# A planner that keeps VectorE's two-operand and double-rate operations apart from GpSimd's, half-height q^T and k^T loads, and other decode priorities

## The chip, the cores and the metric

One core of one Trainium2 chip runs the whole program. The metric is the device time of one execution in microseconds, as the median of three runs. The engines are TensorE (PE for matmuls, PEld for weight loads), VectorE (DVE), ScalarE (ACT) and GpSimd (POOL); SyncE (SP) issues the DMAs.

## The reference

Attention with a memory term, then a two-layer MLP without biases, all in fp32:

```python
B, H, S, D = 8, 8, 576, 64
scores = where(causal, -1e9, q @ k^T / sqrt(D))
a = exp(scores - scores.max(-1));  a /= a.sum(-1) + 1e-9
local = a @ v
phi(x) = where(x > 0, x, exp(x) - 1) + 1
mem = (phi(q) @ M_prev) / (phi(q) @ z_prev + 1e-6)
gate = 1 / (1 + exp(-beta))                     # one number a head
x = (gate * mem + (1 - gate) * local)           # -> 4608 tokens x 512
h = x @ w_in;  g = h - tanh(h);  out = g @ w_out  # w_in 512 x 2048, w_out 2048 x 512
```

## The kernel before

**Attention.** The 64 heads (8 batches of 8) are taken one after the other, t = 0 to 63, in 32 pairs; `EPV = 4`, the first four pairs (heads 0 to 7), use plain fp32 matmuls, the later ones a split of each operand into a rounded high part and a remainder (fp32r), so that a product is two or three fast matmuls. For one head: `scores` makes S = qK^T in four chunks of 128 queries and 192, 320, 448 and 576 keys (PE, line 191, into the PSUM tiles psS and psA); `masked` (DVE, L321) adds the causal mask, writes P and takes the row's extreme into nm; ACT (L223) takes the exponential and sums it into nm. `scale_phi` works on four numbers a row: `nm <- nm,eb` (DVE, L279), `nm <- nm,nr` (DVE, L259) and `rs <- nm` (L329); then two fills `P <- ph,nm` (128x128, DVE or POOL) put the memory term into the same P, so that one product with v and M makes both. `transp` transposes P in blocks (PE, L199), ACT casts the result to pt's high part (L235), DVE subtracts for the remainder (`pt <- psA,pt`, L259); `pv` multiplies by v; `scale_x` and `store_x` scale x^T and write it to DRAM.

For each pair: `load_qk` brings q^T and k^T into qk (head 0 and head 1 side by side; the host has laid the 64 rows of each out twice, on 128 partitions), `qx` and `kx` are the high copies (ACT, DVE or POOL), the lower half of qx (`qx <- qk,qx`, 64x1024) and kz (64x1152) the remainders, `vs` the split of v; `prep_phi` makes ph and nr (`nr <- nr,enbx` among it).

**Weights.** w_in and w_out come as raw 8-byte words and are decoded on the chip in chunks of 512 KB: one `TENSOR_SCALAR` (DVE, L279), two integer `SCALAR_TENSOR_TENSOR` (DVE, L303), an absolute value (ACT L297 or DVE), one more `SCALAR_TENSOR_TENSOR`, then the high copy wi/wo and its remainder. The 14 chunks of the first half of the hidden units (phase A: `FCA = 7` of w_in, 7 of w_out) are decoded during attention, raw data in the buffers xr and ot, temporaries dt and dg; `PRI_I` and `PRI_O` give each chunk's place in units of the head number t. The 18 chunks of the second half (phase B; buffers rawB, tB, gB, two of each) can only start when attention's buffers are released, about 712 us into the span.

**MLP.** `feed(0)` does phase A for 12 blocks of 384 tokens, laid between the heads (`LAG = 20`, `PACE = 5`); `feed(1)` does phase B alone after it. In a block, x is split (`xh` the copy, `xl <- xr,xh` the remainder, 128x384 four times); each of the 7 or 9 hidden units of 128 is 12 matmuls into psM, a tanh on ACT, `g <- psM,t` on DVE, the copy gh and the remainder `gl <- g,gh`; then 3 output tiles of 21 or 27 matmuls each.

**The order.** All of this is recorded as a list of operations with options (engine, modelled cost, the call). `Plan.run` builds the order: `_schedule` steps a model clock and gives each engine the ready operation of best rank; `_latest` runs the result backwards to get the next ranks; of `PASSES = 4` the best is written out as the instruction streams. Where an operation may run on several engines, DVE is charged `BIAS = 1000` ns. The model's numbers set only the order and the engine of each operation; on the chip each engine runs its stream in order and waits by semaphores.

## Time and profile before

| quantity | before |
|---|---|
| median of 3 runs (lowest to highest) | 1264.38 us (1262.83 to 1265.12) |
| profiled execution | 1263.97 us |
| its span, first to last instruction | 1262.1 us |
| mean granted PE clock | 0.992 |
| busy: PE, DVE, ACT, POOL | 1197.9, 794.8, 680.3, 644.4 us |

The span has five stages that the text below uses: 0 to 90 us (heads 0 to 7, plain fp32), 90 to 374 us (heads 8 to 35, with 9 of the 14 decoded chunks and the first phase-A work), 374 to 712 us (heads 36 to 63 with most of phase A), 712 to 840 us (the rest of phase A and the decoding for phase B), 840 us to the end (phase B). A PE that is busy is not yet a PE at its best, because matmul ends are modelled; its waits are listed by what released them.

### The profile page before, as it was taken

To read this page: it belongs to the slowest core of one execution; us is meant where nothing else is said; L and a number is where in the kernel's file an instruction comes from. 1 tells how busy PE (TensorE), PEld (TensorE's weight loads), DVE (VectorE), ACT (ScalarE), POOL (GpSimd) and SP (SyncE) were. 2 spreads that over 40 slices of the span, in tenths; PEclk is the share of its full clock that TensorE was granted. 3 is DMA by queue.
4 is the path that set the end of the run, shared out by engine and by line. 5 is a ranking of instruction groups with operands and counts; after the bars stand their busy time and mean duration, and the time that the engine had idled before them with its cause. 6 is when DMAs were issued, how large, how long until landed. Compare 5 with 4: busy or idle time off the path is not lost.

```text
span 1262.1 us, 18668 instructions
## 1 busy us (share of the span) xinstructions
PE 1197.9 (95%) x6496; PEld 1045.3 (83%) x6496; DVE 794.8 (63%) x1663; ACT 680.3 (54%) x1523; POOL 644.4 (51%) x655
## 2 busy tenths in 40 slices
PE   7998778999999999999999989899999999999998
PEld 4457667978898988898989877789999888999987
DVE  4789999999988897887986588622221222222121
ACT  4778766878876776676765445423332222333221
POOL 2548887867755565665656256533332223333221
PEclk9999889999999999999999999999999999999999
DMA  5655535455343343353330354202212221221200
GB/s 175 191 182 162 167 119 186 130 163 159 116 165 114 115 145 115 88 167 118 120 110 22 141 168 167 84 31 70 75 53 74 76 67 34 76 75 51 75 25 26
DMA packets 71999, 138.85 MB, mean 110 GB/s; under 512 B 18272, under 2 KB 42848, under 8 KB 71904
## 3 DMA queue, kind: packets, MB, share of 16 engines
q1 hardware_dynamic: 71904, 137.65, 33.8%
q8 instruction: 51, 0.84, 0.3%
q14 instruction: 44, 0.36, 0.1%
HBM read 109.32 MB, written 28.31 MB: 109 GB/s over the span
## 4 chain that ended last, share of the span: by engine, by line
PE 44%; DVE 7%; issue 1%; DMA 1%; ACT 1%; POOL 0%; SPq 0%; DVEq 0%; ACTq 0%
PE psM L191 41%; PE psA L191 2%; PE psA L199 1%; DVE tB L303 1%; DVE gB L303 1%; DMA rawB<-in_moe_w_in_dram 1%; DVE g L259 1%; DVE pt L259 1%; DVE tB L279 0%; DVE xl L259 0%; DVE P L321 0%; PE psS L191 0%; DMA vm<-in_vm_dram 0%; DVE gl L259 0%; ACT gB L297 0%
## 5 line engine op out<-in xcount | busy, mean ns | idle before, releaser
L191 PE MATMUL psM<-xh,wi 128*128 128x384 f32 x1536 | 414.9, 340 | 7.2 <-DVE g L259 6.3
L264 POOL TENSOR_TENSOR gl<-g,gh 128x384 fp32r<-128x384 f32 x161 | 171.4, 1065 | 327.8 <-ACT gh L235 326.4
L191 PE MATMUL psM<-wo,gh 128*128 128x512 f32 x1008 | 323.1, 396 | 0.8 <-DVE g L259 0.8
L191 PEld LDWEIGHTS psM<-xh,wi 128*128 128x128 f32 x1536 | 278.7, 188 | 12.2 <-DVE g L259 9.2
L191 PE MATMUL psM<-xl,wi 128*128 128x384 f32 x768 | 259.3, 338 | 0.0
L223 ACT ACTIVATE t<-psM 128x384 f32<-128x384 f32 x192 | 93.8, 490 | 249.2 <-PE psM L191 248.9
L191 PEld LDWEIGHTS psM<-wo,gh 128*128 128x128 f32 x1008 | 187.6, 189 | 36.1 <-DVE g L259 1.5
L259 DVE TENSOR_TENSOR g<-psM,t 128x384 f32<-128x384 f32 x192 | 105.7, 551 | 168.5 <-ACT t L223 168.4
L191 PE MATMUL psM<-wo,gl 128*128 128x512 f32 x504 | 199.4, 396 | 6.1 <-DVE gl L259 6.1
L223 ACT ACTIVATE P<-P,nm 128x448 f32<-128x448 f32 (+3 forms) x256 | 157.6, 617 | 41.9 <-DVE nm L321 41.3
L199 PE MATMUL psA<-ident,P 128*128 128x128 f32 x874 | 142.3, 281 | 14.3 <-DVE pt L259 6.5
L199 PEld LDWEIGHTS psA<-ident,P 128*128 128x128 f32 x874 | 107.1, 143 | 47.9 <-issue 12.8
L191 PEld LDWEIGHTS psM<-xl,wi 128*128 128x128 f32 x768 | 144.6, 188 | 1.2
L191 PE MATMUL psA<-pt,vs 128*128 128x512 f32 (+3 forms) x560 | 136.5, 351 | 7.3 <-DVE pt L259 4.3
L259 DVE TENSOR_TENSOR pt<-psA,pt 128x512 fp32r<-128x512 f32 x224 | 133.9, 610 | 6.9 <-ACT pt L235 6.4
L259 DVE TENSOR_TENSOR ot<-psM,pin 128x512 f32<-128x512 f32 x36 | 24.9, 692 | 178.1 <-PE psM L191 178.1
L235 ACT CAST pt<-psA 128x512 fp32r<-128x512 f32 x224 | 116.5, 531 | 35.9 <-PE psA L199 34.4
L235 ACT CAST gh<-g 128x384 fp32r<-128x384 f32 x144 | 73.9, 513 | 85.4 <-DVE g L259 85.0
L191 PEld LDWEIGHTS psM<-wo,gl 128*128 128x128 f32 x504 | 95.2, 189 | 26.2 <-DVE gl L259 7.8
L191 PEld LDWEIGHTS psA<-pt,vs 128*128 128x128 f32 x560 | 93.9, 192 | 19.9 <-DVE pt L259 7.1
L321 DVE CUSTOM_DVE_ANT_0 P<-psS,mask 128x576 f32<-128x576 f32 (+1 forms) x96 | 67.5, 703 | 20.9 <-PE psS L191 20.5
L321 DVE CUSTOM_DVE_ANT_0 P<-psA,mask 128x320 f32<-128x320 f32 (+2 forms) x160 | 68.8, 453 | 18.2 <-PE psA L191 16.7
(155 smaller groups left out, 1858.8 us busy)
## 6 DMA issues: line engine op xcount, KB each, us to landing
qk<-in_qk_dram SPq DMA_DIRECT2D x61, 576.0 KB, 4.0
xr<-xs SPq DMA_DIRECT2D x23, 768.0 KB, 4.4
qn<-in_qn_dram SPq DMA_DIRECT2D x32, 320.0 KB, 3.1
vm<-in_vm_dram SPq DMA_DIRECT2D x30, 320.0 KB, 3.4
part<-ot SPq DMA_DIRECT2D x12, 768.0 KB, 4.1
pin<-part SPq DMA_DIRECT2D x12, 768.0 KB, 5.8
out_dram<-ot SPq DMA_DIRECT2D x11, 768.0 KB, 4.2
rawB<-in_moe_w_in_dram SPq DMA_DIRECT2D x9, 512.0 KB, 3.8
```

Source lines behind the costliest of these rows:

```text
L191: [("PE", n * c / 2.4 + 13, lambda: nc.tensor.matmul(real(out), lhsT, rhs, start=start, stop=stop))],
L199: [("PE", self._n(out) * 2 / 2.4 + 3, lambda: nc.tensor.transpose(real(out), in_, ident))],
L223: [("ACT", c, lambda: nc.scalar.activation(out=out, in_=real(in_), func=func, **kw))],
L235: "ACT", n / 1.2 + (51 if ps else 93), lambda: nc.scalar.copy(out, real(in_))
L259: lambda: nc.vector.tensor_tensor(out=out, in0=real(a), in1=b, op=op),
L264: lambda: nc.gpsimd.tensor_tensor(out=out, in0=a, in1=b, op=op),
L303: [("DVE", self._n(out) / 0.96 + 65, lambda: nc.vector.scalar_tensor_tensor(out=out, in0=real(a), scalar=s, in1=b, op0=op0, op1=op1))],
L321: [("DVE", self._n(out) / 0.96 + 77, lambda: nc.vector.tensor_tensor_reduce(out=real(out), in0=real(in_), in1=mask, scale=-scale, scalar=3 ...
```

## The change

1. In the planner, a resource "port" is added. Every POOL option holds it, and every DVE option that reads more than one SBUF operand of more than one element a row, or that is a copy, a tensor-scalar or an absolute value with its source in SBUF (`fast`). An operation that needs the port is not placed while another one holds it, in the forward and in the backward pass. BIAS stays.
2. `load_qk` for pairs 0 to 3 brings 64 rows a head in two DMAs (head h on partitions 64h to 64h+63, 64x576 each) in place of one of 128x1152; `scores` reads the head's own partitions. The ring `r_qe` becomes four half tiles of qk; a part of ot is no longer used for it, and pair 4 uses the common ring.
3. `PRI_I` and `PRI_O`, the places of the phase-A chunks, become earlier, and the raw buffers of phase A alternate strictly between xr and ot.

```diff
-PRI_I = (-1.0, -1.0, 8.0, 11.2, 12.0, 12.8, 13.6)
-PRI_O = (10.0, 10.3, 10.6, 10.9, 11.2, 11.5, 11.8)
+PRI_I = (-1.0, -1.0, 3.0, 4.0, 5.0, 6.0, 7.0)
+PRI_O = (7.5, 8.0, 8.5, 9.0, 9.5, 10.0, 10.5)
...
-    def add(self, opts, reads, writes, tail=0.0):
+    def add(self, opts, reads, writes, tail=0.0, fast=False):
...
+        sb = sum(not isinstance(x, View) and x.space != DRAM and self._n(x) > 1 for x in reads)
+        opts = [
+            o + (o[0] == "POOL" or (o[0] == "DVE" and (fast or sb > 1)),) for o in opts
+        ]
...
-        self.add(opts, r, [out])
+        self.add(opts, r, [out], fast=a.space != PSUM)
...
                         best = min(
-                            max(free[x[0]], now) + x[1] + self.bias.get(x[0], 0.0)
-                            for x in op["opts"]
+                            max(free[x[0]], free["port"] if x[3] else 0.0, now) + x[1]
+                            + self.bias.get(x[0], 0.0) for x in op["opts"]
                         )
...
-                    take = self._fits(op, now)
+                    take = None if o[3] and free["port"] > now else self._fits(op, now)
...
                     end = free[e] = now + o[1]
+                    if o[3]:
+                        free["port"] = end
...
-    r_raw.t = r_xr.t + (r_xr.t + r_ot.t) * FCA
+    r_raw.t = r_xr.t + r_ot.t
...
-    r_qe.t = r_qk.t + [r_ot.t[0][:, 0:2 * S].rearrange("p (h s) -> p h s", h=2)]
+    r_qe.t = [t[:, h] for t in r_qk.t for h in range(2)]
...
-        d["raw"] = (r_qe if pr <= EPV else r_qk).next()
-        pl.dma(d["raw"], qk[b, p, :, w], False)
+        if pr < EPV:
+            d["raw"] = r_qe.next()
+            for h in range(2):
+                a = slice(64 * h, 64 * h + 64)
+                pl.dma(d["raw"][a], qk[b, p, a, w, h], False)
+        else:
+            d["raw"] = r_qk.next()
+            pl.dma(d["raw"], qk[b, p, :, w], False)
...
-            terms = ((qx[0:64, h], kx[0:64, h]),)
+            a = slice(64 * h, 64 * h + 64)
+            terms = ((qx[a], kx[a]),)
```

The order on SP at the start of the program, before; qk_111 and qk_112 are the two buffers for q^T and k^T:

```order
L673 DMA bt<-in_beta_dram 128x8
L336 DMA qk_111<-in_qk_dram 128x1152
L336 DMA qk_112<-in_qk_dram 128x1152
L336 DMA qn_109<-in_qn_dram 128x640
L336 DMA z_121<-in_z_prev_dram 128x128
L336 DMA vm_110<-in_vm_dram 128x640
L336 DMA ot_169<-in_qk_dram 128x1152
```

and after:

```order
L690 DMA bt<-in_beta_dram 128x8
L341 DMA qk_111<-in_qk_dram 64x576 x2
L341 DMA qn_109<-in_qn_dram 128x640
L341 DMA z_121<-in_z_prev_dram 128x128
L341 DMA qk_111<-in_qk_dram 64x576 x2
L341 DMA xr_159<-in_moe_w_in_dram 128x4x256
L341 DMA vm_110<-in_vm_dram 128x640
```

The k^T of the first pair is now issued sixth and seventh, behind qn and z, where it was third; a raw chunk of w_in goes out ahead of v.

The order on DVE around the first P of the 17th head (psS,mask 128x576), before; dt and dg are the decode's temporaries, xr and ot its raw data:

```order
L303 SCALAR_TENSOR_TENSOR dt_165<-dg_166,dt_165 128x512
L279 TENSOR_SCALAR nm_148<-nm_148,eb 128x4
L279 TENSOR_SCALAR dt_164<-ot_169 128x512
L321 ISA P_145,nm_147<-psS,mask 128x576
L321 ISA nm_147 128x1
L259 TENSOR_TENSOR nm_148<-nm_148,nr_129 128x4
L303 SCALAR_TENSOR_TENSOR dg_166<-ot_169,dt_164 128x512
L259 TENSOR_TENSOR xT_144<-psA_154,tmp_151 64x512
L329 RECIPROCAL rs_150<-nm_147 128x4
L303 SCALAR_TENSOR_TENSOR dt_164<-ot_169,dg_166 128x512
```

and after:

```order
L326 ISA P_145,nm_147<-psS,mask 128x576
L326 ISA nm_147 128x1
L326 ISA P_145,nm_147<-psA_155,mask 128x192
L326 ISA nm_147 128x1
L326 ISA P_145,nm_147<-psA_155,mask 128x320
L326 ISA nm_147 128x1
L264 TENSOR_TENSOR pt_116<-psA_153,pt_115 128x512
```

No decode operation is left between this head's operations. Counted by the number of heads whose 128x576 operation stands ahead of a chunk's first operation, the 14 chunks start at 3 5 6 7 8 10 12 14 14 15 15 15 16 17 before and at 2 2 3 4 5 7 8 8 10 10 12 13 14 15 after: eight of them stood at 12 to 17 heads, now four do. Over the whole program DVE has 1589 rows where it had 1665, ACT 1303 (1269), POOL 702 (660), SP 376 (368), PE the same 6354. To POOL go 40 `xl`, so that all 92 are there, 19 `P <- ph,nm`, so that all 128 are there, 7 gl and 6 kz; 8 of the qx remainders go from POOL to DVE, and a few dozen copies (vs, qx, xh, gh) from POOL to ACT.

The order on DVE in the transition at 712 us, before; rawB, tB and gB belong to phase B's decoding, g to phase A:

```order
L259 TENSOR_TENSOR g_163<-psM_156,t_161 128x384
L279 TENSOR_SCALAR tB_6681<-rawB_6679 128x512
L303 SCALAR_TENSOR_TENSOR gB_6683<-rawB_6679,tB_6681 128x512
L303 SCALAR_TENSOR_TENSOR tB_6681<-rawB_6679,gB_6683 128x512
L259 TENSOR_TENSOR g_162<-psM_157,t_160 128x384
L303 SCALAR_TENSOR_TENSOR tB_6681<-gB_6683,tB_6681 128x512
L279 TENSOR_SCALAR tB_6682<-rawB_6680 128x512
L259 TENSOR_TENSOR g_163<-psM_156,t_161 128x384
```

and after:

```order
L264 TENSOR_TENSOR g_162<-psM_157,t_160 128x384
L264 TENSOR_TENSOR g_163<-psM_156,t_161 128x384
L308 SCALAR_TENSOR_TENSOR tB_6690<-gB_6692,tB_6690 128x512
L284 TENSOR_SCALAR tB_6689<-rawB_6687 128x512
L284 TENSOR_SCALAR tB_6690<-rawB_6688 128x512
L308 SCALAR_TENSOR_TENSOR gB_6691<-rawB_6687,tB_6689 128x512
L308 SCALAR_TENSOR_TENSOR gB_6692<-rawB_6688,tB_6690 128x512
L308 SCALAR_TENSOR_TENSOR tB_6689<-rawB_6687,gB_6691 128x512
L308 SCALAR_TENSOR_TENSOR tB_6690<-rawB_6688,gB_6692 128x512
L308 SCALAR_TENSOR_TENSOR tB_6689<-gB_6691,tB_6689 128x512
L308 SCALAR_TENSOR_TENSOR tB_6690<-gB_6692,tB_6690 128x512
L284 TENSOR_SCALAR tB_6689<-rawB_6687 128x512
```

Decode operations that stood one or three at a time between two g now stand in runs of two chunks, mostly where PE works on output tiles and no g is due. Before, all 18 chunks began ahead of phase A's last tile; now the last of them begin when phase B's first block has begun.

## The prediction

> **What bounds the kernel now.** I read the page's slices first, then the span cut into its five stages, then PE's waits in each stage, and last the durations of single operations on the engine that those waits name.

> ```profile
> PE   7998778999999999999999989899999999999998
> DVE  4789999999988897887986588622221222222121
> PEclk9999889999999999999999999999999999999999
> ```

> PE is the fullest engine nearly everywhere; DVE is full only from slice 4 to 11, where the granted clock dips as well. The stages (columns: length, then busy us of PE, PE weight loads, DVE, ACT, POOL, then granted clock, DMA share, GB/s):

> ```profile
> 0.00:90.00 90.00, 81.05 (x315) 43.46 (x315) 59.62 (x159) 58.88 (x134) 40.35 (x60) 1.00 0.57 179
> 90.00:374.00 284.00, 255.18 (x1516) 221.07 (x1516) 271.04 (x613) 216.93 (x501) 212.56 (x210) 0.97 0.49 154
> 374.00:712.00 338.00, 327.13 (x1969) 296.49 (x1968) 272.15 (x625) 229.41 (x535) 191.72 (x209) 0.99 0.34 108
> 712.00:840.00 128.00, 116.16 (x580) 103.08 (x579) 90.42 (x115) 59.46 (x116) 73.32 (x58) 1.00 0.41 138
> 840.00:1262.00 422.00, 418.33 (x2122) 381.17 (x2121) 101.54 (x154) 115.63 (x238) 126.41 (x119) 1.00 0.18 59
> ```

> In the last stage PE is busy 418.3 of 422 us: nothing but fewer or faster matmuls shortens it, and the change leaves the matmuls as they are. In the second, 90 to 374 us, DVE is busy 271.0 of 284 us, 95%, and PE loses 28.8; in the third DVE is at 80.5% and PE loses 10.9. What PE waits for in the second stage (PE tile, line, releaser: total us, times, longest; 12 rows that add to 28.2):

> ```profile
> PE psA L199 <- DVE pt L259: 5.5, 6, 1.5
> ...
> PE psA L199 <- DVE P L259: 1.9, 1, 1.9
> ...
> PE psS L191 <- POOL P L264: 0.6, 1, 0.6
> ```

> Nearly all of it is DVE, and spread over many tiles: DVE is short of time as a whole. Why it is so full stands in the durations of its smallest work (shortest/median/longest ns):

> ```profile
> L279 DVE TENSOR_SCALAR nm<-nm,eb x64: 208/230/3027, 17.5 to 697.5; 128x4 f32<-128x4 f32 x64
> L259 DVE TENSOR_TENSOR nm<-nm,nr x64: 142/165/1682, 21.3 to 697.7; 128x4 f32<-128x4 f32 x64
> L303 DVE SCALAR_TENSOR_TENSOR nr<-nr,enbx x32: 131/161/1805, 20.8 to 661.9; 128x10 f32<-128x10 f32 x32
> L259 DVE TENSOR_TENSOR g<-psM,t x192: 491/557/560, 102.6 to 1240.6; 128x384 f32<-128x384 f32 x192
> L264 POOL TENSOR_TENSOR qx<-qk,qx x21: 2357/2401/3415, 94.0 to 649.8; 64x1024 fp32r<-64x1024 f32 x21
> L259 DVE TENSOR_TENSOR xl<-xr,xh x40: 519/1002/1372, 204.6 to 1203.3; 128x384 fp32r<-128x384 f32 x40
> L264 POOL TENSOR_TENSOR xl<-xr,xh x52: 1002/1028/2189, 202.9 to 1204.2; 128x384 fp32r<-128x384 f32 x52
> ```

> An operation on four numbers a row that takes 0.2 us at best takes up to 3.0, about as long as POOL's longest operations (2.4 us, at worst 3.4). `g`, with one operand in PSUM, never exceeds 0.56 us in 192 cases. So DVE operations of the class that the change marks "port" stand still while POOL works, and the time counts as DVE busy. In the second stage the groups average (busy us, mean ns):

> ```profile
> L279 DVE TENSOR_SCALAR nm<-nm,eb 128x4 f32<-128x4 f32 x28 | 19.3, 688 | 0.3
> L259 DVE TENSOR_TENSOR nm<-nm,nr 128x4 f32<-128x4 f32 x28 | 14.4, 513 | 0.0
> L303 DVE SCALAR_TENSOR_TENSOR dt<-dg,dt 128x512 f32<-128x512 f32 x10 | 8.8, 878 | 0.0
> L303 DVE SCALAR_TENSOR_TENSOR nr<-nr,enbx 128x10 f32<-128x10 f32 x14 | 7.4, 527 | 0.0
> L303 DVE SCALAR_TENSOR_TENSOR dg<-xr,dt 128x512 int32<-128x512 int32 x5 | 5.4, 1070 | 0.0
> L303 DVE SCALAR_TENSOR_TENSOR dt<-xr,dg 128x512 int32<-128x512 int32 x5 | 5.0, 1008 | 0.0
> L279 DVE TENSOR_SCALAR dt<-xr 128x512 int32<-128x512 int32 x5 | 3.2, 637 | 0.0
> ```

> Standing still costs (688-208)x28 = 13.4, (513-142)x28 = 10.4 and (527-131)x14 = 5.5: 29 us from these three groups alone.

> **The change part by part.** *Port in the planner, second stage.* The model now places such an operation when POOL is free, and moves two-operand work (40 xl, 19 P fills, 7 gl and 6 kz in the whole program) to POOL. On the chip the two streams keep only their order, and durations differ from the model's, so they drift: I take two thirds of the 29 us, 20. A decoded chunk costs DVE 637 + 1070 + 1008 + 878 ns = 3.6 us, and three of the nine leave this stage by the new priorities: 11 us. DVE falls from 271 to 240 us. The PE loss at a given DVE load is read from the two stages: 28.2 us of 284 (9.9%) at 95.4% and 10.9 of 338 (3.2%) at 80.5%, 0.45 points a point. With a length of 273 the load is 87.9%, the loss 6.5% or 17.8 us, and 284 - 28.2 + 17.8 = 273.6 closes the circle: -10 us. What would be late next is PE's own 255.8 us, so this term lies between 0 (DVE's relief is not where PE waits) and -28.

> *The clock in the second stage.* The lowest slices are in the stretch where eight of the fourteen chunks were decoded:

> ```profile
> 120.00:140.00 20.00, 16.70 (x96) 13.23 (x94) 19.94 (x45) 16.49 (x38) 18.51 (x15) 0.92 0.62 192
> 140.00:160.00 20.00, 15.50 (x84) 12.66 (x84) 19.94 (x39) 14.45 (x31) 16.13 (x15) 0.91 0.61 184
> 160.00:180.00 20.00, 15.52 (x70) 12.42 (x71) 19.98 (x38) 12.38 (x26) 16.78 (x13) 0.83 0.46 142
> ```

> DVE has 0.02 to 0.06 us free of 20 there, PE is busy 75 to 84% by modelled ends, and the clock is 0.83 to 0.92. With 3% of 284 us missing in the stage's mean clock, 8.5 us is the most that a full clock could give, 0 the least. The drops go with the decode bunch, which is thinned from eight chunks to four but not gone; I take -2, near the lower end, since the rows at 0.91 and at 0.83 have the same PE load, so load alone does not set it. [...]

> *First stage.* The three chunks put 11 us more on DVE in 0 to 90, which is busy 59.6 of 90 us. PE's waits there (first and last of 3 rows, 8.9 us together):

> ```profile
> PE psS L191 <- DMA qk<-in_qk_dram: 7.0, 1, 7.0
> ...
> PE psA L199 <- DVE xT L259: 0.4, 1, 0.4
> ```

> Only 1.9 us of these are DVE's, so its 30 us of slack cover the chunks on average; if the cover is gone where a chunk falls ahead of a head's P, up to one chunk, 3.6 us, shows. The 7.0 us before the first matmul is a load:

> ```profile
> L336 SPq DMA_DIRECT2D qk<-in_qk_dram x61: 327/333/547, 1.2 to 631.8; - x61
> ```

> An issue takes SP 0.33 us. k^T is now the sixth and seventh issue where it was the third, so it leaves 4 x 0.33 = 1.3 us later, with half the bytes in each. The halved bytes can give back at most some of the 7.0 us. I set the stage at 0, between -4 and +4. That pairs 0 to 3 have four half tiles lets a k load go earlier; PE does not wait for any qk load after the first, so it is 0.

> *Third stage.* The largest of its 6 rows of PE waits, and the last:

> ```profile
> PE psS L191 <- DVE nm L321: 6.1, 5, 3.0
> ...
> PE psA L199 <- DVE xT L259: 0.2, 1, 0.2
> ```

> No chunk is decoded here, so only the port acts: between 0 and -10.9; by the same two thirds of the one DVE-late group, -4.

> *Transition, 712 to 840 us.* PE waits 11.8 us, all for DVE, and DVE's decoding stands still too: (1179 - 683) x 18 = 8.9 us for one of its four operations (whole-run shortest, median, longest; then the stage's busy and mean):

> ```profile
> PE psM L191 <- DVE g L259: 6.0, 9, 1.2
> PE psM L191 <- DVE gl L259: 5.8, 3, 2.0
> L303 DVE SCALAR_TENSOR_TENSOR gB<-rawB,tB x18: 683/1351/1662, 719.0 to 804.4; 128x512 int32<-128x512 int32 x18
> L303 DVE SCALAR_TENSOR_TENSOR gB<-rawB,tB 128x512 int32<-128x512 int32 x18 | 21.2, 1179 | 0.2
> ```

> The three gl that PE waited for go to POOL, and the decode runs stand where no g is due. Against it, the last chunks start after phase B's first block has begun, so their wo may be late for its output tiles. Between -11.8 and +8 (two chunks of 3.6 us, which nothing hides then); I take -4, the gl row less what POOL's slower gl gives back.

> *Phase B.* All xl on POOL: one takes 1.03 us where DVE's median is 1.00, four a block of about 35 us of PE work, and PE has no listed wait in this stage: 0.

> Sum: 0 - 10 - 2 - 4 - 4 + 0 = -20 us. The profiled execution took 1263.97 us, 0.4 under the median, for a span of 1262.1; 1263.97 - 20 = 1244. With half and one and a half times of it this gives 1254 and 1234.

> **The rivals.** *Relief is complete.* If DVE keeps ahead of PE everywhere, 28.2 + 10.9 + 11.8 = 50.9 us go: 1213. For it: these waits are short, so a little slack could end many at once. Against: at 80.5% DVE load PE still lost 10.9 us.

> *The planner's apartness does not last on the chip.* Streams drift, stretched operations stay as they are, and only the 11 us of moved chunks count: DVE at 260 of 280 us, loss 8.7%, -4: 1260. For it: the three small groups stand behind other DVE work in an in-order stream and start when that ends, not when POOL pauses. The stretch is then also partly what hides POOL's time.

> *The transition pays.* As the forecast, but with +8 in place of the -4 there: 1244 + 12 = 1256. For it: wo's chunks are now the last to be decoded. Against: PE waited for no wo before.

> *Slower: POOL becomes late.* All 128 `P <- ph,nm` are on POOL, two a head, behind xl, kz or qx of 1.0 to 2.4 us in its in-order stream, and transposes of P wait for them. In 56 heads a mean delay of 20/56 = 0.36 us a head cancels the gain; at 0.5 us, half an xl, it is 28 us, or 1244 + 28 = 1272. For it: POOL gets more work, and DVE did 19 fills at 0.29 us median where POOL needs 0.40:

> ```profile
> L264 POOL TENSOR_TENSOR P<-ph,nm x109: 389/402/1516, 22.1 to 698.3; 128x128 f32<-128x128 f32 x109
> L259 DVE TENSOR_TENSOR P<-ph,nm x19: 229/291/1300, 197.0 to 689.4; 128x128 f32<-128x128 f32 x19
> POOL gl L264 <- ACT gh L235: 326.4, 103, 18.5
> ```

> Against it: PE waited for a POOL fill once, 0.6 us, though POOL did 109 of them, and POOL stands 326 us of the run waiting only for gh, so it has room. [...]

> **How the numbers follow.** A change of 0.2% (2.5 us) is about what can be told from none. The forecast has 0.48 (1244, own range 1234 to 1254), complete relief 0.10 (1213), the paying transition 0.08 (1256), lost apartness 0.19 (1260, with a spread that puts 0.06 of it within 0.2% of before), POOL late 0.15 (1272). Faster: 0.48 + 0.10 + 0.08 + 0.13 = 0.79; the same 0.06; slower 0.15. The range goes from 1213, which keeps the complete case, to 1267, the unrelieved sum with the first stage's +4 (1264 + 4, rounded down), and leaves out most of the slower case.

> **What would show it.** Right: in the second stage DVE busy near 240 us with `nm <- nm,eb` at a mean of about 0.37 us, PE waits of about 18 us, phase B unchanged at 422 us, and no xl above 1.1 us in the median. Wrong: those small operations still at 0.6 us or more (drift), PE waiting for POOL's P or kz (POOL late), PE waiting for woB or wo remainders at the start of phase B (transition), or a first matmul more than 2 us later than before.

## The result, and the profile after

The changed kernel takes 1234.67 us (median of 4 runs, 1231.45 to 1236.06) against 1264.75 us: a ratio of 0.9761, 95% interval 0.9739 to 0.9783, or 30 us. Forecast were 1244 us, with 1213 to 1267 as the range. The profiled execution, the slowest of the four, took 1236.06 us for a span of 1234.3 us.

The page's slices of the kernel after:

```profile
PE   8998889989999999999999999999999999999998
DVE  5889989889798778786876557721122111122111
PEclk9999989989999999999999999999999999999999
```

DVE no longer stands at 9 from slice 4 to 11 (counted from 1), but the clock row has dips as before. The stages, with the columns of the same view before (length; busy us of PE, PE loads, DVE, ACT, POOL; clock, DMA share, GB/s). To compare work with work, the bounds here are landmarks, events of PE that every run has: the end of the 128x576 scores of head 8 and of head 36, the last transpose, the first of the 2268 matmuls of phase B:

```profile
0.00:86.70 86.70, 81.58 (x317) 43.90 (x318) 64.28 (x168) 62.94 (x144) 38.57 (x54) 1.00 0.61 176
86.70:364.90 278.20, 254.08 (x1497) 221.18 (x1496) 247.86 (x578) 220.79 (x506) 194.14 (x201) 0.95 0.46 146
364.90:693.50 328.60, 324.86 (x1979) 297.63 (x1979) 246.88 (x604) 236.75 (x550) 210.18 (x241) 0.99 0.36 115
693.50:783.90 90.40, 88.53 (x441) 78.78 (x441) 58.89 (x79) 46.43 (x91) 56.01 (x47) 1.00 0.49 168
783.90:1234.30 450.40, 446.64 (x2269) 407.07 (x2268) 97.96 (x160) 131.55 (x269) 160.45 (x157) 1.00 0.18 61
```

By the same landmarks the kernel before has 89.6, 284.3, 336.6 and 101.9 us, and phase B takes 445.9 us of matmuls before and 446.6 after. So 3 us went in the first stage, 6 in the second, 8 in the third, 11.5 in the transition: less than a quarter of the gain is where DVE was fullest.

Even these 6 us are not a shorter stage. At head 36 PE ran 7.5 us ahead of DVE after the change, and 19 matmuls fewer stand in its second stage (1497, before 1516), 18 more in its third (1979, before 1961). Counted from DVE's first P to first P, with nearly the same work in each, the second stage is 1.5 us longer, 284.1 to 285.6, and heads 36 to 63 take 305.0 us where they took 320.3. PE's waits after, in the second stage (10 rows, 23.7 us together; 28.2 before):

```profile
PE psA L204 <- DVE pt L264: 8.7, 5, 3.3
PE psA L196 <- DVE xT L264: 3.7, 4, 1.5
...
PE psA L196 <- DVE pt L264: 0.4, 1, 0.4
```

They are fewer (22, before 33), but the longest is longer than before (3.3 us, 1.9 before). In the third stage and in the transition nearly nothing is left (3.8 and 1.6 us; 10.9 and 11.8 before). All rows, the first three of the third stage, the last two of the transition:

```profile
PE psA L196 <- DVE pt L264: 2.5, 1, 2.5
PE psM L196 <- DVE g L264: 1.0, 1, 1.0
PE psS L196 <- DVE nm L326: 0.3, 1, 0.3
PE psM L196 <- DVE g L264: 1.2, 2, 0.7
PE psM L196 <- ACT ot L240: 0.4, 1, 0.4
```

### The profile page after: what moved, and what is told of

Same layout as the page of the kernel before. It is cut to its first block, busy times and chain, and to the rows that moved or that the text cites. A ratio compares the mean times of both kernels' runs of the same rounds, so it can differ in the third digit from the quotient of the medians.

```text
span 1234.3 us, 18697 instructions
## 1 busy us (share of the span) xinstructions
PE 1195.7 (97%) x6496; PEld 1048.6 (85%) x6496; DVE 715.9 (58%) x1587; ACT 698.5 (57%) x1557; POOL 659.4 (53%) x697
## 3 DMA queue, kind: packets, MB, share of 16 engines
q1 hardware_dynamic: 72032, 135.29, 34.1%
## 4 chain that ended last, share of the span: by engine, by line
PE 84%; DVE 9%; ACT 2%; issue 2%; DMA 1%; POOL 1%; SPq 0%; ACTq 0%; DVEq 0%; POOLq 0%
PE psM L196 58%; PE psA L196 14%; PE psA L204 8%; PE psS L196 4%; DVE nm L284 2%; DVE pt L264 1%; DVE tB L308 1%; DVE P L326 1%; DVE xT L264 1%; DVE qx L264 1%; ACT P L228 1%; DVE g L264 1%; DMA qk<-in_qk_dram 1%; DMA rawB<-in_moe_w_in_dram 1%; DVE dt L308 0%
## 5 line engine op out<-in xcount | busy, mean ns | idle before, releaser
L269 POOL TENSOR_TENSOR gl<-g,gh 128x384 fp32r<-128x384 f32 x168 | 177.9, 1060 | 309.2 <-ACT gh L240 290.5
L264 DVE TENSOR_TENSOR g<-psM,t 128x384 f32<-128x384 f32 x192 | 106.2, 553 | 184.6 <-ACT t L228 182.2
L264 DVE TENSOR_TENSOR pt<-psA,pt 128x512 fp32r<-128x512 f32 (+1 forms) x224 | 135.6, 616 | 26.2 <-ACT pt L240 25.0
L240 ACT CAST pt<-psA 128x512 fp32r<-128x512 f32 (+1 forms) x224 | 116.3, 531 | 54.3 <-PE psA L204 47.4
L264 DVE TENSOR_TENSOR ot<-psM,pin 128x512 f32<-128x512 f32 x36 | 24.9, 691 | 185.5 <-PE psM L196 185.5
L240 ACT CAST gh<-g 128x384 fp32r<-128x384 f32 x150 | 77.1, 514 | 75.9 <-DVE g L264 75.6
L196 PEld LDWEIGHTS psM<-wo,gl 128*128 128x128 f32 x504 | 95.4, 189 | 18.3
L269 POOL TENSOR_TENSOR xl<-xr,xh 128x384 fp32r<-128x384 f32 x92 | 95.2, 1048 | 4.7 <-ACT xh L240 4.5
L269 POOL TENSOR_TENSOR P<-ph,nm 128x128 f32<-128x128 f32 x128 | 59.6, 484 | 59.7 <-DVE nm L264 26.6
```

Of the source, the lines that this page charges most:

```text
L196: [("PE", n * c / 2.4 + 13, lambda: nc.tensor.matmul(real(out), lhsT, rhs, start=start, stop=stop))],
L240: "ACT", n / 1.2 + (51 if ps else 93), lambda: nc.scalar.copy(out, real(in_))
L264: lambda: nc.vector.tensor_tensor(out=out, in0=real(a), in1=b, op=op),
L269: lambda: nc.gpsimd.tensor_tensor(out=out, in0=a, in1=b, op=op),
```

## The experiments

All times are medians of 4 to 15 runs. Stage lengths by the same landmarks, from one profiled execution each (for e12 the fastest of its four, 1206.6 us); the last two columns are PE's waits in the second stage and the time at half rate in it, in us:

| kernel | median us | ratio to before | to head 8 | heads 8 to 36 | to last transpose | transition | waits | half rate |
|---|---|---|---|---|---|---|---|---|
| before | 1264.75 | 1 | 89.6 | 284.3 | 336.6 | 101.9 | 28.2 | 17.1 |
| after | 1234.67 | 0.976 [0.974, 0.978] | 86.7 | 278.2 | 328.6 | 90.4 | 23.7 | 27.3 |
| e1 port alone | 1245.02 | 0.984 [0.983, 0.985] | 88.5 | 295.4 | 321.0 | 90.4 | 31.7 | 34.1 |
| e2 decode alone | 1271.62 | 1.006 [1.004, 1.007] | 85.4 | 296.7 | 337.1 | 103.3 | 36.1 | 17.1 |
| e3 loads alone | 1261.24 | 0.998 [0.997, 0.999] | 90.9 | 279.8 | 335.6 | 103.4 | 31.3 | 6.8 |
| e4 after, latency 260 | 1216.22 | 0.961 [0.960, 0.963] | 85.3 | 264.9 | 320.5 | 90.8 | 14.5 | 6.8 |
| e5 choice alone | 1257.90 | 0.995 [0.993, 0.997] | 93.3 | 274.4 | 334.3 | 102.3 | 25.6 | 17.1 |
| e6 apart alone | 1234.03 | 0.976 [0.975, 0.978] | 86.5 | 275.3 | 328.5 | 90.3 | 23.8 | 20.5 |
| e7 before, latency 260 | 1270.59 | 1.005 [1.003, 1.007] | 86.0 | 294.2 | 334.7 | 104.5 | 32.3 | 23.9 |
| e8 after, nm on ACT | 1207.03 | 0.955 [0.953, 0.957] | 88.1 | 255.2 | 322.9 | 90.6 | 10.1 | 0 |
| e9 e8, latency 260 | 1212.22 | 0.958 [0.956, 0.959] | 83.7 | 266.5 | 320.3 | 90.6 | 13.5 | 10.2 |
| e10 before, nm on ACT | 1269.95 | 1.004 [1.003, 1.005] | 92.1 | 287.8 | 335.1 | 103.6 | 30.8 | 19.3 |
| e11 after, qx and kz cut | 1213.89 | 0.959 [0.958, 0.961] | 82.5 | 266.1 | 322.2 | 90.4 | 12.7 | 10.2 |
| e12 e8 and e11 | 1211.51 | 0.956 [0.954, 0.958] | 87.4 | 256.5 | 320.1 | 90.4 | 14.2 | 3.4 |

Two things stand in this table. The transition is 90.3 to 90.8 us in every kernel whose planner keeps port operations apart and 101.9 to 104.5 in every other; the third stage 320 to 329 against 334 to 337. The second stage runs from 255 to 297 us in no such order, and the first from 82.5 to 93.3. But the second stage's length less the waits and less half of the half-rate time (granted clock 0.50 in the windows below) is 240 to 252 us in all fourteen: 284.3 - 28.2 - 8.5 = 247.6 before, 278.2 - 23.7 - 13.7 = 240.8 after, 264.9 - 14.5 - 3.4 = 247.0 in e4, 255.2 - 10.1 - 0 = 245.1 in e8.

**e1, the port rule alone.**

```diff
 # before, with add(), _schedule and _latest of the change
 PRI_I = (-1.0, -1.0, 8.0, 11.2, 12.0, 12.8, 13.6)
 r_raw.t = r_xr.t + (r_xr.t + r_ot.t) * FCA
 d["raw"] = (r_qe if pr <= EPV else r_qk).next()
```

> Before, with the planner's port resource alone (the decode priorities, raw buffers and q, k loads as before). Theory A, the port rule makes the gain of the third stage (320.3 to 305.0 us between the first P of head 36 and of head 63) and of the transition (101.9 to 90.4 us between the last transpose and phase B): 1264.8 - 15 - 11 = about 1238, with the first stage at 90 us as before. Rival B, the decode priorities make it by clearing DVE early, so that all later work is less pressed: no more than 10 us here, above 1254. Rival C, any new order of this planner moves the time by tens of us at random: no forecast, anywhere from 1230 to 1270.

1245.0 us. Its third stage and transition (the last two of these windows; the first is heads 8 to 36):

```profile
88.50:383.90 295.40, 262.98 (x1526) 229.85 (x1525) 253.77 (x603) 230.83 (x524) 213.04 (x212) 0.94 0.48 149
383.90:704.90 321.00, 320.11 (x1959) 293.87 (x1958) 242.18 (x586) 231.21 (x541) 215.32 (x236) 1.00 0.35 112
704.90:795.30 90.40, 88.55 (x442) 78.77 (x441) 58.77 (x79) 46.46 (x91) 56.02 (x47) 1.00 0.49 167
```

The gain of both later stages is there: the transition takes the 90.4 us of the kernel after, and between the DVE landmarks named in the expectation it is 305.0 us, as there. So B falls: the priorities are not needed for it. The total missed the 1238 by 7, all of it in the second stage, which is 11 us longer than before at a clock of 0.94.

**e2, the decode priorities alone.**

```diff
-PRI_I = (-1.0, -1.0, 8.0, 11.2, 12.0, 12.8, 13.6)
+PRI_I = (-1.0, -1.0, 3.0, 4.0, 5.0, 6.0, 7.0)
-PRI_O = (10.0, 10.3, 10.6, 10.9, 11.2, 11.5, 11.8)
+PRI_O = (7.5, 8.0, 8.5, 9.0, 9.5, 10.0, 10.5)
-r_raw.t = r_xr.t + (r_xr.t + r_ot.t) * FCA
+r_raw.t = r_xr.t + r_ot.t
```

> Before, with the new decode priorities and the alternating raw buffers alone. Theory A: the chunks leave the crowded stretch at 120 to 175 us, the second stage gains up to 5 us, the third stage and the transition stay at 320 and 102 us: 1258 to 1266. Rival B: 1240 to 1250, with the later stages shorter too. Rival C: anywhere.

1271.6 us: slower, outside A's range and far from B's. The later stages stayed, as A said; the second stage grew by 12 us where it was to gain up to 5.

**e3, the 64-row loads alone.**

```diff
-        d["raw"] = (r_qe if pr <= EPV else r_qk).next()
-        pl.dma(d["raw"], qk[b, p, :, w], False)
+        if pr < EPV:  # two DMAs, head h on partitions 64h to 64h + 63
...
-            terms = ((qx[0:64, h], kx[0:64, h]),)
+            terms = ((qx[a], kx[a]),)
```

> Before, with the 64-row q and k loads of the first four pairs alone. If the 1.9 us by which the first matmul came earlier after the change (5.1 us, before 7.0) is the smaller first load, it is here too, and the first P of head 8 comes at 86 to 88 us, not 90: 1260 to 1263 in all. If it came from the order of the other loads, the first stage stays at 90 us and the time at 1264 to 1265. Rival C: anywhere.

1261.2 us. The first wait of PE in e1, which has the old loads, and in e3:

```profile
PE psS L196 <- DMA qk<-in_qk_dram: 7.0, 1, 7.0
PE psS L191 <- DMA qk<-in_qk_dram: 5.0, 1, 5.0
```

The half-height load lets the first matmul start 2 us earlier. That head 8 comes earlier by it was wrong: it came at 90.9 us, 1.3 later than before, with 84.2 us of PE work ahead of it where there were 80.7. The time fell into the forecast range all the same, by a second stage 4.5 us shorter, which nothing in this edit was to change: the number came out, its reason did not.

One reading of the start order, that the first pair's k^T is issued later, was wrong. The loads of 64x576 bring one head's q^T or k^T each, and the first two are the first head's q^T and k^T (kernel after: start, us, engine, operation):

```profile
1.19 1.22 SPq L341 DMA_DIRECT2D qk<-in_qk_dram  x2
3.55 1.11 SPq L341 DMA_DIRECT2D qk<-in_qk_dram  x2
5.12 2.25 PE L196 MATMUL psS<-qk 64*128 64x288 f32 x4 [5.12 <-DMA qk<-in_qk_dram]
```

The first two have landed at 4.25 and 4.98 us and the first matmul waits for these alone; the sixth and seventh issue, the second head's q^T and k^T, land at 7.4 and 8.2 us. So the first head's k^T is still issued third, with half the bytes, and was not put off.

**e4, another order and nothing else.**

```diff
-LAT = 250.0
+LAT = 260.0
```

> After, with the planner's modelled latency between engines at 260 ns in place of 250: nothing of the change is touched, only ties and near ties in the order fall out another way. Theory A: 1230 to 1240, with the second stage up or down by the chance places of its half-rate clock windows (3.4 us each, 8 after, 5 before). Rival C: over 10 us away from 1234.7.

1216.2 us, 18 us faster than the kernel after by 10 ns in a model constant. It is neither A (1230 to 1240) nor a chance of the whole order: transition and phase B stayed within 0.4 us, and heads 36 to 63 take 304.3 us from first P to first P (305.0 after). The first stage differs by 1.4 us; the rest is the second stage, with 1538 matmuls in 264.9 us where the kernel after has 1497 in 278.2, and the clock at 0.99:

```profile
85.30:350.20 264.90, 249.87 (x1538) 220.71 (x1538) 239.60 (x587) 228.94 (x522) 202.96 (x208) 0.99 0.52 161
```

**e5 and e6, the port in the engine choice alone, and in the placing alone.** e5 takes out the two places that hold an operation back, e6 the one that weighs engines:

```diff
 # e5
-                    take = None if o[3] and free["port"] > now else self._fits(op, now)
+                    take = self._fits(op, now)
-                    while heaps[e] and port[heaps[e][0][1]] and free["port"] > now:
+                    while False and heaps[e]:
 # e6
-                            max(free[x[0]], free["port"] if x[3] else 0.0, now) + x[1]
+                            max(free[x[0]], now) + x[1]
```

> After, but the planner looks at the port only when it weighs the engines of one operation against each other; it may place a port operation while another holds the port, forward and backward. Theory A1, keeping apart makes the gain: the third stage is back near 318 us and the transition near 102, where the change alone had 305 and 90; about 1255 to 1265, give or take the second stage's 15. Theory A2, the engine choice makes it: 305 and 90 stay, 1220 to 1240.

> After, but the port is left out where the planner weighs the engines of one operation against each other; it still places no port operation while another holds the port. A1: third stage 305, transition 90 us, 1220 to 1245 by the second stage's chance. A2: 318 and 102, above 1250.

A1 holds in both: e6 is the kernel after (1234.0), e5 has the stages of before (third stage and transition):

```profile
367.70:702.00 334.30, 326.25 (x1961) 294.71 (x1959) 268.01 (x619) 230.24 (x536) 193.05 (x210) 0.99 0.34 107
702.00:804.30 102.30, 90.03 (x442) 78.60 (x441) 83.87 (x104) 48.36 (x94) 61.60 (x47) 1.00 0.48 162
```

DVE's 268 and 84 us there stand against 247 and 59 after.

What the two runs separate is the places in the planner's code, not two effects on the chip. The rule in the placing does two things at once: it keeps port operations apart, and as DVE is held back it moves operations to POOL. All eight kernels with that rule have all 92 xl, 128 fills and 168 gl on POOL; the six without it, e5 too, have 39 to 41 xl, 13 to 21 fills and 7 to 10 gl on DVE. Whether the gain is that DVE has less to do or that the rest is undisturbed needs a kernel with the engines of after and no holding back. None was run.

**e7, before with the latency at 260 ns.** The same edit as e4, in the kernel before.

> Before, with the planner's modelled latency at 260 ns in place of 250. If only the second stage depends on the chance of the order (it went from 265 to 297 us in the runs so far), the third stage stays at 318 to 321 us and the transition at 102 to 104, and the time is 1250 to 1280. If the whole order is a matter of chance (rival C), the third stage or the transition moves by more than 5 us.

1270.6 us, with 294.2 us in the second stage, here 10 us in the other direction. The third stage is 318.0 us between DVE's landmarks, as forecast, and the transition 104.5, half a microsecond over; the first stage moved too, by 3.6 us. So the early stages are open to chance and the later ones are not. The -30 us of the change thus hold a draw on each side: with 260 ns in both planners the same change is worth 54 us (1270.6 to 1216.2). What both pairs show is the third stage by DVE's landmarks (-15.3 and -13.7) and the transition (-11.5 and -13.7), 27 us together each time.

**e8, nm <- nm,eb on ACT.** One of the waits that the second stage kept, in the timeline after (start, us, engine, operation; in brackets the wait ahead of it):

```profile
249.02 3.50 POOL L269 TENSOR_TENSOR kz<-qk,kx 64x1152 fp32r<-64x1152 f32 x1
250.04 4.00 DVE L284 TENSOR_SCALAR nm<-nm,eb 128x4 f32<-128x4 f32 x1
252.49 1.52 POOL L269 TENSOR_TENSOR vs<-vm,vs 128x640 fp32r<-128x640 f32 x1
253.96 0.54 DVE L264 TENSOR_TENSOR pt<-psA,pt 128x384 fp32r<-128x384 f32 x1
254.65 1.09 PE L204 MATMUL psA<-ident,P 128*128 128x128 f32 x4 [2.93 <-DVE pt L264]
```

A product of four numbers a row stands through two POOL operations, pt behind it in DVE's stream is late, and PE waits 2.9 us. The operation becomes ready when ACT's last exponential ends, and in the second stage it fared worse than before, while the other two small groups fared better (kernel after, second stage; 688, 513 and 527 ns before):

```profile
L284 DVE TENSOR_SCALAR nm<-nm,eb 128x4 f32<-128x4 f32 x27 | 23.9, 884 | 1.4 <-ACT P L228 1.4
L264 DVE TENSOR_TENSOR nm<-nm,nr 128x4 f32<-128x4 f32 x27 | 8.2, 303 | 0.0
L308 DVE SCALAR_TENSOR_TENSOR nr<-nr,enbx 128x10 f32<-128x10 f32 x13 | 2.2, 172 | 0.1
```

```diff
-        pl.ts(sm, sm, 1e-9, eb[:, hh:hh + 1], ALU.add, ALU.mult)
+        pl.ts(sm, sm, eb[:, hh:hh + 1], None, ALU.mult, None, "A")
```

> After, with the product nm <- nm,eb on ACT (the addition of 1e-9 is left out, which a sum of at least 1 does not show in fp32), so that the one small DVE operation that stands still longest (mean 0.87 us in the second stage, once 4.0 us, with PE waiting 3.3 us behind it) leaves the port. Theory: of the 18 us that it stood still in the second stage PE gets a good part back, and fewer half-rate windows follow (8 there now): second stage down from 278 to 262 to 270 us, the rest as after, 1215 to 1228. Rival: ACT, in order, brings rs later and the transposes wait for it, or the order falls out worse by chance: 1235 or more.

1207.0 us, better than forecast, and the fastest of all: 27.6 us under the kernel after, of which 23 in the second stage (30 between DVE's landmarks). That stage, and the first two of PE's waits in it:

```profile
88.10:343.30 255.20, 244.92 (x1537) 218.76 (x1536) 229.43 (x556) 226.05 (x542) 210.09 (x211) 1.00 0.52 162
PE psA L196 <- DVE nm L326: 2.2, 4, 0.9
PE psA L204 <- DVE pt L264: 2.2, 3, 1.8
```

No half-rate window is left in attention, and no wait is over 1.8 us. But e4 gained 18 us by another order alone, so one run does not show how much of this is the operation's.

**e9, the same with the latency at 260 ns.**

> After with nm <- nm,eb on ACT, as in the run before, and the planner's modelled latency at 260 ns. If that run's 1207 came from the op's leaving the port, it is here too: no more than two half-rate windows during attention, second stage 250 to 262 us, 1203 to 1216. If it came from a lucky order, this falls back to the runs with the op on DVE: 1216 to 1235.

1212.2 us, inside the range, but the two other conditions failed: the second stage is 266.5 us and has three half-rate windows (10.2 us). It is 4 us under e4, its counterpart with the operation on DVE, yet the second stage, which the move was to shorten, is 264.9 us in e4 with 6.8 at half rate, so it gained nothing there. e8 is 27.6 us under its own counterpart. That the move helps beyond the chance of the order is therefore not shown.

**e10, nm on ACT in the kernel before.** The edit of e8 without the port rule.

> Before (no port in the planner) with nm <- nm,eb on ACT alone. If that one operation is most of what the port costs in the second stage, this stage falls from 284 to 260 to 275 us, and the third stage and the transition stay at 316 to 321 and 102 to 104 us, because the port rule made those: 1240 to 1256. If it helps only together with the rule: 1258 to 1268.

1270.0 us, above both ranges: the forecast failed. The operation left the port (0.30 us each on ACT), yet DVE was still busy 273.6 of 287.8 us (the ACT row from 88 to 372 us, the two DVE rows below it from 88 to 360):

```profile
L283 ACT ACTIVATE nm<-nm,eb 128x4 f32<-128x4 f32 x27 | 8.1, 299 | 0.1
L259 DVE TENSOR_TENSOR vs<-vm,vs 128x640 fp32r<-128x640 f32 x6 | 12.3, 2048 | 0.1
L259 DVE TENSOR_TENSOR qx<-qk,qx 64x1024 fp32r<-64x1024 f32 x6 | 11.8, 1960 | 0.6 <-POOL qx L245 0.5
92.10:379.90 287.80, 256.47 (x1514) 220.80 (x1515) 273.62 (x589) 223.45 (x529) 210.61 (x211) 0.97 0.49 154
```

The planner put other work on DVE in its place: before, two vs and one qx stood there from 88 to 360 us, 4.2 us in all, now twelve operations of 24.1 (and seven kz fewer, 9.4 us where there were 17.9). So the run does not show what this one operation cost before; that it matters more where the rule holds, because the rule cannot place it, is a guess.

**e11, the remainders of qx and kz cut in two**, and **e12, both edits.**

```diff
-        pl.tt(kz[0:64], raw[0:64], kx[0:64].bitcast(F32), ALU.subtract, "PV")
+        for h in range(2):
+            pl.tt(kz[0:64, h], raw[0:64, h], kx[0:64, h].bitcast(F32), ALU.subtract, "PV")
...
+        for h in range(2):
+            pl.tt(qx[lo, h], raw[lo, h], qx[lo, h].bitcast(F32), ALU.subtract, "PV")
```

> After, with the two longest remainders, qx (64x1024, 2.4 us on POOL) and kz (64x1152, 2.7 us), each cut into one operation a head, so that the port is held half as long at a time; nm <- nm,eb stays on DVE. If the length of POOL's operation sets how long it stands still, its mean falls from 0.87 us in the second stage to 0.5 to 0.7, and its longest from 4.0 to about 2.5 us: 1215 to 1232. If only the number of meetings counts, no change or, by the 56 more instructions' fixed cost, slower: 1235 to 1242.

> After, with both: nm <- nm,eb on ACT and the remainders of qx and kz cut in two. With no half-rate window left in attention and 10 us of PE waits in the second stage, little is left to win: 1200 to 1210. If shorter holds also free pt and P on POOL, the second stage falls below 252 us.

e11 took 1213.9 us. Whole run, shortest, median and longest of the small product:

```profile
L284 DVE TENSOR_SCALAR nm<-nm,eb x64: 163/574/2125, 16.8 to 657.9; 128x4 f32<-128x4 f32 x64
```

Its longest fell from 4.0 to 2.1 us, but its median rose from 0.23 to 0.57, and its mean in the second stage from 0.88 only to 0.76 us, where 0.5 to 0.7 was forecast: it stands more often, each time shorter. The cut did more than shorten: all 56 halves of kz and all 56 of qx went to POOL, where the kernel after has 14 kz and 15 qx on DVE. The time fell by 21 us, but e4 fell by 18 by another order alone, so that the cut is the cause is not shown. e12, at 1211.5, is just outside its range and no better than e8, and its second stage is not under 252 us.

## Why the prediction was right, and where its steps were off

The direction and the range held, and so did the mechanism in the large: with the rule in the placing (e6 against e5) PE's waits in the second to fourth stage fell from 50.9 to 29.1 us, nearly all of them waits for DVE. The slower rival did not come: no wait of PE for POOL's P or kz is among the rows after, with all 128 fills there. The transition cost nothing, and phase B stayed. But the terms were placed wrongly, and the errors cancelled: 12 us were forecast for the second stage, where 6 came by PE's landmarks and none by DVE's, and 8 for the third stage and the transition, where 20 to 27 came. That the total was only 10 us off is in part luck, and the second stage's share of it is a draw.

Of the signs named beforehand, those of the later stages held: phase B as before, a median xl of 1.02 us, an earlier first matmul. In the second stage DVE came to 248 us, not 240, PE's waits to 23.7, not 18, and `nm <- nm,eb` to a mean of 0.88 us, not 0.37. That is over the 0.6 us set as the sign of drift, so in this stage the rival of lost apartness was right about the largest of the three groups.

- *Port, second stage: -10 forecast; the whole stage -6 by PE's landmarks, +1.5 by DVE's, and +11 with the port alone (e1).* The step that failed is "two thirds of the 29 us". The three groups took 41.1 us before and, in the rows shown with e8, 34.3 after: 7 us given back, not 20, because `nm <- nm,eb` got worse. The three chunks did leave the stage (7 of the last decode operation stand there, before 10). DVE fell by 23 us instead of 31, to 248. The loss-by-load line itself was not far off: 247.9 of 278.2 is 89.1%, for which it gives 7.1% or 19.7 us; 23.7 were measured.
- *Clock: -2 forecast, about +5 measured* (27.3 instead of 17.1 us at half rate; a half of the difference is the estimate). The step took the dips for a matter of the decode bunch. In the traces the eight stretches at half rate in this stage, three before and five after, each follow 3.41 us in which PE was busy for 13 to 55% (below), seven of them with one wait of PE of 1.7 to 3.3 us there; and the waits became fewer (22, before 33) and the longest longer (3.3 us, before 1.9).
- *Third stage: -4 forecast, -8 measured by PE's landmarks, -15 by DVE's; -16 in e1 and e4.* The step priced only the DVE-late wait and left out what its own list of moved work does there: DVE lost 11 xl, 14 P fills and two kz there. Before (first three) and after:

```profile
L259 DVE TENSOR_TENSOR kz<-qk,kx 64x1152 fp32r<-64x1152 f32 x8 | 16.2, 2030 | 1.0 <-ACT kx L235 1.0
L259 DVE TENSOR_TENSOR xl<-xr,xh 128x384 fp32r<-128x384 f32 x11 | 6.7, 614 | 0.0
L259 DVE TENSOR_TENSOR P<-ph,nm 128x128 f32<-128x128 f32 x14 | 5.9, 446 | 0.0
L264 DVE TENSOR_TENSOR kz<-qk,kx 64x1152 fp32r<-64x1152 f32 x6 | 8.6, 1425 | 0.0
```

  These are 20 of the 25 us by which DVE's busy time fell (272.2 to 246.9). By the means before, about 17 of the 20 are operations that left DVE, the rest is that kz took less time. PE's waits went down to 3.8 us, in e1 to 0.9.
- *Transition: -4 forecast, -11.5 measured.* Nearly the whole of PE's 11.8 us of waits went. The term took the gl row alone and left out the 6.0 us of waits for g. The decode itself got hardly shorter (its four operations took 65.9 us before, 63.3 after). The waits for gl ended with its move to POOL; that those for g ended because the decode now stands where no g is due is read from the order, not tested. The late wo, +8 as an end, did not show: PE has no listed wait in phase B.
- *First stage: 0 forecast, -3 measured.* PE's waits fell from 8.9 to 5.1 us: 1.9 by the halved first load, which e3 has too, and 1.9 by two waits for DVE that are gone. The later k^T that the step set against it does not exist, since the first head's k^T kept its place (e3). That the 1.9 us reach head 8 is not shown: in e3 they did not.
- *The priorities* were credited with 11 us of DVE relief in the second stage. Alone they made the kernel 0.6% slower (e2), by the second stage; what they add to the port rule (1245 to 1235, with the loads) is no more than the chance of that stage, and stays open.

## What to carry to other kernels

A planner that models a resource as exclusive should do so in the placing, not only in the choice of an engine: here the one gave the gain of the later stages (e6, 1234.0 us), the other nothing that they show (e5, 1257.9 us). A tiny operation that becomes ready at a moment no plan controls can still stand for 4 us (`nm <- nm,eb`, 4.00 us at 250 us into the span); on ACT it took 0.30 us each and 0.33 at most (all 64 in e10), but what it was worth in time was not told from chance. And before a gain of a few per cent from a list scheduler is believed, move a constant that means nothing: here that was worth 18 us and 6 us, and the stage table showed which part of the gain was no chance, some 27 us in the later stages.

## What the runs showed of the hardware

```profile
167.50:170.91 3.41, 1.54 (x9) 0.90 (x7) 3.41 (x4) 1.76 (x4) 3.33 (x3) 1.00 0.51 147
170.91:177.74 6.83, 6.15 (x22) 5.36 (x22) 6.83 (x18) 4.33 (x11) 4.92 (x4) 0.50 0.69 218
250.24:253.65 3.41, 1.47 (x7) 0.87 (x5) 3.41 (x1) 2.30 (x4) 3.41 (x2) 1.00 0.54 173
253.65:260.48 6.83, 5.83 (x20) 5.20 (x21) 5.08 (x17) 2.96 (x8) 2.07 (x4) 0.50 0.46 144
```

PE was busy 45% and 43% of the 3.41 us ahead (by modelled matmul ends). Ahead of all ten stretches it was busy for 0.44 to 1.88 us of 3.41, 13 to 55%, so in none of them was it idle throughout. With both traces divided into windows of 3.41 us from these starts: of 22 full-rate windows with PE busy under 60%, ten were followed by half rate, and twelve, at 44 to 60%, were not; of the 673 others, none was. Of 15 half-rate windows, the five with PE busy for 68 to 81% were followed by another one, the ten from 85% on by full rate. These are counts of two traces; what lowers the clock is not shown by them. As an estimate from the clock of 0.50, 3.41 us at half rate cost up to 1.7 us where PE has work, so each of the two stretches above up to 3.4 us, on top of the longest wait ahead of it (1.9 and 2.9 us).
